# Loading the first batch's k through SyncE in float32 and casting it on the engines, with a new written order, in a kernel of sparse attention and a gated feed-forward

## The chip, the cores and the metric

The kernel runs on one core of one Trainium2 chip. The core has five engines that each follow their own list of instructions: TensorE (PE; its weight loads are shown as PEld), VectorE (DVE), ScalarE (ACT), GpSimd (POOL) and SyncE (SP). Data moves between the chip's memory (HBM) and the core's on-chip memory (SBUF) by DMA, on 16 DMA engines. A DMA is issued by an instruction on POOL or on SP. In this kernel POOL issues every load, and those loads also cast float32 to bfloat16 on the way; SP issues the output stores and small moves inside the core's memory. TensorE writes its results to PSUM.

The metric is the time of one execution in device microseconds (us), the median of several runs.

## The reference

```python
def _attn_ref(q, k, v):                      # B, H, S, D = 4, 8, 768, 64
    block, window = 32, 16
    k_sum = k.reshape(B, H, nb, block, D).max(axis=3)
    v_sum = v.reshape(B, H, nb, block, D).mean(axis=3)
    scores_l = scale * q @ k^T               # kept only where |i - j| < window
    scores_s = scale * q @ k_sum^T + log(block)
    a = softmax over both together
    return a @ concatenate([v, v_sum])
def _moe_ref(x, w_in, w_out):                # x: 3072 x 512, w_in: 512 x 2048
    h = x @ w_in
    return (h * clip(h + 3, 0, 6) / 6) @ w_out
```

Each position attends to the keys less than 16 places away, and to one summary key (the maximum) and one summary value (the mean) of each of the 24 blocks of 32 positions. The heads' outputs are put side by side, and the 3072 rows of 512 go through a feed-forward part with a gated hidden layer of 2048. Inputs and output are float32; the matmuls run in bfloat16.

## The kernel before

**Attention.** Heads go in pairs (four pairs p per batch). For a tile t of 64 queries, the keys are a window of 96 positions and the 24 summary keys, 120 in all. `kaug[p]` holds the transposed keys of pair p by tile, `qT` the transposed queries, `vaug` the values. Scores are computed in halves of six tiles, ACT takes the exponential into `at`, DVE multiplies by a mask (or PE adds a bias first), PE multiplies by the values, DVE normalizes, and PE transposes the result into `x`.

**The first batch.** Batch 0 has its own path. `load_k` (L303) loads k of one or two pairs into `knat` with a casting DMA issued by POOL; 96 partitions hold 8 successive positions of each head. `load_q` (L309) does the same for half of q. Both lie in the tile `first`. `k_step` (L383) transposes k of one pair on PE, DVE takes the block maximum, and ACT or DVE copy the windows into `kaug`. The other half of q comes through `qwide` (`load_wide`, L316): four DMAs. The values come through `load_v` (L339), one DMA per pair. Batches 1 to 3 are loaded in another layout into `kraw`, `qraw` and, for batch 2, again into `first`.

**Feed-forward.** The 3072 rows are eight tiles s of 384. For each, sixteen chunks ft of 128 hidden units: PE multiplies four times (L666), ACT makes the gate (L670), DVE multiplies (L671) into `g`. Then `f2` multiplies `g` by `w_out` (L683), ACT or DVE copy the result out of PSUM, and SP stores it. `w_in` is loaded in five pieces (`load_w`, L371; tokens I0, I2, I4, I8, I12, each holding the chunks from that number up to the next piece: two chunks in I0 and I2, four in the others), `w_out` in four (`load_w2`, L376; tokens O0 to O3). They stay on chip.

**The order.** Nothing is scheduled by the engines themselves. The kernel lists its operations with their dependencies, and a long text, `ORDER`, says in which order they are issued; each engine takes its own in that order. A token such as `k1.2:A` is the operation number 2 of the step k1, put on ACT (`:D` is DVE). The step letters that matter here: K0p load k of pair p; Q0g load q; V0p load values; Q0wu load wide q; k and q the steps that transpose them; s0ph scores of batch 0, pair p, half h; u block sums of the values; h halo copies of values; v0p the values' product for pair p; Fsxft the hidden chunk ft of row tile s (for the first five chunks of tile 0 its four matmuls are four operations, .0 to .3); Gstsx0 the second product; c the constants. Tokens that start with `_`, `-`, `~` or `=` are dummy matmuls on a tile of ones, which fill time in which PE would otherwise be idle (40 of 64 columns for `_40`, 15 of 128 for `-15`, 12 of 512 for `~12`, one of 64 times n for `=n`).

A transfer is waited for by the engine whose next instruction needs it. DMAs issued by POOL share eight completion counters in turn, so that each also waits for the eighth DMA before it.

Of the kernel before, what the change touches and what calls it, by code (L numbers as in the profile page):

```python
# [29 lines left out]
c.0 K00.0 c.7 c.17 c.6 c.8:A K01.0 c.10:D c.5 c.1 _40 -15 k0.0 k0.2:A c.18 ~1 =2 k1.0 K02.0 ~12 =3 k2.0 k3.0 c.15:D c.2 c.3  # L30
s000.0 k0.3:A c.13:D c.4 c.11:A k1.1 Q00.0 q0.0 k1.4 k0.1 c.20 k1.2:A Q01.0 ~2 =5 q1.0 k0.4 k1.3:D c.9:A c.14:A c.19 k2.3:A
q0.1:A s000.1 q0.2:A =1 s010.0 s010.1 k2.2:A k3.2:D k3.3:D k3.1 V00.0 h000.0:D h001.0:D k2.1 k2.4 s000.2 ~2 =5 v00.0 V01.0 u0.0
h010.0:D s020.0 c.16 s010.2 q1.2:A u0.3:D u0.1:D u0.4:D v01.0 v01.1 v01.2 v00.1 q1.1:A V02.0 h020.0:A h021.0:A h011.0:A v00.2
s020.1 v01.3 v00.3 V03.0 u1.0 u1.3:A h030.0:D s030.0 k3.4 ~2 s030.1 u1.4:D v01.4 h031.0:D Q0w0.0 Q0w1.0 v01.5:D Q0w2.0 =1 q3.0
q3.1:D q2.0 u1.1:A u1.2:D s020.2 v02.0 v02.1 v02.2 s021.0 v02.3 s030.2 v03.0 v03.1 q2.1:A v03.2 s011.0 v03.3 v00.4 v00.5:D v02.4
s021.1 s011.1 s021.2 v03.4 v03.5:D s011.2 v02.5:A s031.0 s031.1 s001.0 s031.2 I2.0 F0x3.0 F0x3.1 F0x3.2 F0x3.3 F0x3.4 F0x3.5
I4.0 F0x6.0 F0x6.1 F0x6.2 F0x4.0 F0x4.1 F0x4.2 F0x4.3 v411.0 v411.1 F0x5.0 F0x4.4 F0x4.5 v411.2 s001.1 I8.0 u0.2:A s001.2 F0x8.0
F0x8.1 F0x8.2 F0x5.1 I0.0 F0x5.2 F0x11.0 F0x1.0 F0x11.1 F0x11.2 F0x1.1 F0x1.2 F0x1.3 F0x1.4 F0x1.5 v410.0 v410.1 F0x7.0 F0x7.1
F0x7.2 v410.2 F0x10.0 F0x10.1 I12.0 F0x13.0 F0x13.1 F0x15.0 F0x15.1 F0x13.2 F0x10.2 v411.3 v411.4:D v410.3 v410.4:A F0x15.2
F0x14.0 F0x14.1 F0x14.2 F0x9.0 F0x9.1 F0x9.2 F0x0.0 F0x0.1 F0x2.0 F0x2.1 K13.0 K10.0 c.12:A F0x0.2 K12.0 K11.0 w10.0 Q1w1.0  # L40
F1x14.0 F1x14.1 F1x14.2 F1x4.0 F1x4.1 F1x4.2 F1x2.0 F1x2.1 F1x2.2 w10.1:D F0x2.2 F0x2.3 F0x2.4 F0x12.0 F0x12.1 F0x12.2 F1x8.0
F1x8.1 F1x8.2 F1x1.0 F1x1.1 F1x1.2 F0x0.3 F0x0.4 F0x0.5 F0x2.5 F1x9.0 F1x9.1 F1x9.2 F1x5.0 F1x5.1 F1x5.2 F1x15.0 F1x15.1 w11.0
w11.2 F1x15.2 w11.3:D Q1w4.0 Q1w2.0 Q1w0.0 w10.2 w10.3:D q6.0 q6.1:A q7.0 q7.1:A F1x7.0 F1x7.1 w11.1:A F1x7.2 F1x12.0 F1x12.1
F1x12.2 O0.0 G02x0.0 Q1w5.0 Q1w3.0 q4.0 q4.1:A q5.0 q5.1:A F1x6.0 F1x6.1 F1x6.2 O1.0 G02x0.1 s100.0 s100.1 s100.3 F1x3.0 w12.0
F1x11.0 F1x11.1 w13.0 w13.2 F1x3.1 F1x11.2 w12.2 w12.1:D O2.0 G02x0.2 s101.0 s101.1 O3.0 F1x10.0 G02x0.3 G02x0.4:A w13.3:D
w13.1:A s101.3 F1x0.0 G00x0.0 G00x0.1 w12.3:D s100.2 s101.2 s100.4 V10.0 h100.0:D F1x10.1 h110.0:A F1x10.2 F1x3.2 s110.0 s110.1
s110.2 s101.4 s110.3 G00x0.2 G00x0.3 G00x0.4:A V12.0 u4.0 h130.0:D h120.0:A F1x0.1 u4.1:D u4.2:A u4.4:D u4.3:D u4.5:D G02x0.5
G01x0.0 G01x0.1 G01x0.2 s110.4 F1x0.2 h111.0:A v100.0 v100.1 v100.2 h121.0:A v101.0 v101.1 v101.2 G01x0.3 G01x0.4:A K20.0 K21.0
K22.0 K30.0 K23.0 w21.0 F1x13.0 F1x13.1 F1x13.2 v100.3 v100.4:A w20.0 w21.3 G12x0.0 w21.2:A v101.3 v101.4:A V22.0 H2.0 h101.0:A
w20.3 G12x0.1 G12x0.2 F2x2.0 F2x2.1 F2x11.0 F2x2.2 F2x11.1 F2x11.2 s111.0 w23.0 s111.3 F2x1.0 F2x1.1 F2x1.2 F2x3.0 F2x3.1 F2x3.2  # L50
F2x15.0 F2x15.1 F2x15.2 Q22.0 w23.3 G12x0.3 s111.1 G12x0.4:A F2x5.0 F2x5.1 h131.0:A F2x5.2 F2x6.0 G10x0.0 s111.2 w22.0 w22.3
s111.4 w23.4:A V20.0 H2.1:A K33.0 F2x13.0 F2x13.1 F2x13.2 G10x0.1 F2x6.1 F2x0.0 F2x0.1 F2x0.2 u5.0 u5.1:A u5.5:A F2x6.2 v110.0
v111.0 v111.1 v111.2 Q30.0 F2x4.0 F2x4.1 F2x4.2 Q21.0 Q23.0 Q20.0 w22.4:A F2x10.0 F2x10.1 F2x10.2 F2x12.0 F2x12.1 w20.1 F2x12.2
w22.2:A v110.1 w21.4:A Q33.0 Q32.0 G10x0.2 G01x0.5 G10x0.3 G10x0.4:A v110.2 F2x8.0 F2x8.1 w21.1 w20.2:A F2x9.0 w20.4:A F2x9.1
F2x9.2 u5.2:D F2x14.0 u5.4:D w23.2:A F2x8.2 v111.3 F2x14.1 v111.4:A G11x0.0 G11x0.1 u5.3:D w22.1 v110.3 v110.4:A F2x7.0 F2x7.1
G11x0.2 F3x14.0 F3x14.1 F2x14.2 F2x7.2 F3x14.2 s200.0 s200.1 w23.1 w21.5:A s200.3 G11x0.3 F3x9.0 F3x9.1 F3x9.2 F3x8.0 F3x8.1
F3x8.2 F3x13.0 Q31.0 K31.0 s200.4 s200.2 G11x0.4:A G11x0.5 G12x0.5 s210.0 s210.3 s210.4 s210.1 s210.2 F3x4.0 F3x12.0 G22x0.0
# [104 lines left out]
def kernel(  # L162
# [535 lines left out]
    load_q(0)
    load_k(0, 1)
    load_k(1, 2)  # L700
    load_q(1)
    load_k(2, 4)
# [100 lines left out]
```

## Time and profile before

| what | value |
|---|---|
| median of 3 runs | 217.12 us (217.12 to 217.85) |
| profiled execution | 217.01 us, its span 215.3 us |
| PE busy | 209.4 us, 97% of the span |
| DVE, ACT, POOL busy | 162.5, 136.2, 49.5 us |
| first matmul of the feed-forward part | 24.33 us after the start |
| landed through queue 0 (POOL's loads) | 14.41 MB |
| landed through queue 1 (SP's stores and moves) | 7.87 MB |

The span is the time between the first and the last instruction that the profiler recorded. A row of the timeline has the start, the duration, the engine, the line, the operation, what it writes and reads, and in brackets how long the engine had been idle before and what ended that. In a row by stretches, the numbers after the stretch's length are the busy time of PE, PEld, DVE, ACT and POOL (each with a count of instructions), then the granted clock of PE, how much the DMA engines had in flight, and the GB/s that landed. A GB/s line divides a stretch into 40 slices. In the chain of work that ended last, each row is a start, a duration and what was running. In the groups, the numbers after the bar are busy time and the mean duration of one in ns.

### The profile page before, as it was taken

How to read it: one execution, taken by the hardware profiler on the slowest of the kernel's cores; microseconds unless marked ns; L12 is line 12 of the kernel's file. 1: busy time of each engine (PE TensorE's matmuls, PEld its weight loads, DVE VectorE, ACT ScalarE, POOL GpSimd, SP SyncE). 2: the span in 40 equal slices, each digit the busy share in tenths (PEclk: the TensorE clock that was granted, in tenths of full speed). 3: DMA queues.
4: the chain of work that ended last, by engine and by line, in shares of the span. 5: the costliest groups of instructions: out<-in, count | busy, mean ns of one | idle time of the engine just before them, and what ended most of it. 6: DMA issues, size and time to landing. Idle time of an engine off the chain costs nothing.

```text
span 215.3 us, 6088 instructions
## 1 busy us (share of the span) xinstructions
PE 209.4 (97%) x2548; PEld 119.6 (56%) x2548; DVE 162.5 (75%) x317; ACT 136.2 (63%) x264; POOL 49.5 (23%) x66
## 2 busy tenths in 40 slices
PE   7998999999999999999999999999999999999993
PEld 7556656555555565555555555555555555565442
DVE  6888999999899999898889888987865554640021
ACT  3887878887898988757569696466345355520110
POOL 7977358906652244000000000000000000000000
PEclk9999999999999999999999999999999999999999
DMA  5999999999999999930333233122323300013124
GB/s 74 157 152 188 203 188 170 191 204 161 205 160 192 181 134 150 104 146 12 37 43 137 28 38 107 49 24 32 73 56 48 73 0 29 23 49 122 52 70 150
DMA packets 91580, 22.68 MB, mean 105 GB/s; under 512 B 82208, under 2 KB 88608, under 8 KB 91552
## 3 DMA queue, kind: packets, MB, share of 16 engines
q0 software_dynamic: 62288, 14.41, 72.2%
q1 hardware_dynamic: 29264, 7.87, 15.4%
q8 instruction: 20, 0.33, 0.6%
q14 instruction: 8, 0.07, 0.1%
HBM read 28.82 MB, written 6.29 MB: 163 GB/s over the span
## 4 chain that ended last, share of the span: by engine, by line
PE 86%; DMA 7%; POOL 2%; ACT 2%; DVE 1%; issue 1%; ACTq 0%; POOLq 0%
PE h L666 38%; PE o L683 33%; PE h L683 5%; DMA qwide<-in_q_dram 4%; DMA first<-in_q_dram 3%; PE S L623 3%; PE S L512 3%; PE S L553 1%; ACT vaug L241 1%; POOL first L305 1%; PE S L636 1%; PE S L439 1%; PE S L666 1%; PE h L581 1%; DVE g L671 0%
## 5 line engine op out<-in xcount | busy, mean ns | idle before, releaser
L666 PE MATMUL h<-x,win 128*128 128x384 bf16 x500 | 91.1, 326 | 0.2 <-DVE g L671 0.2
L670 ACT ACTIVATE r<-h 128x384 f32<-128x384 f32 x125 | 58.8, 492 | 38.7 <-PE h L666 36.7
L671 DVE SCALAR_TENSOR_TENSOR g<-r,h 128x384 bf16<-128x384 f32 x125 | 65.7, 546 | 22.7 <-ACT r L670 20.1
L683 PE MATMUL o<-wout,g 128*128 128x512 bf16 x336 | 81.7, 379 | 0.0
L666 PEld LDWEIGHTS <-win 128*128 128x128 bf16 x512 | 48.7, 98 | 35.8 <-issue 0.4
L683 PEld LDWEIGHTS <-g 128*128 128x128 bf16 x400 | 38.4, 98 | 37.6 <-issue 0.3
L520 ACT ACTIVATE at<-S 120x768 bf16<-120x768 f32 x24 | 18.6, 811 | 5.5 <-PE S L512 5.4
L241 ACT COPY ot<-o 128x512 f32<-128x512 f32 x17 | 10.0, 586 | 16.3 <-PE o L683 15.1
L521 DVE TENSOR_TENSOR at<-at,mask 96x768 bf16<-96x768 bf16 x24 | 12.6, 549 | 2.0 <-ACT at L520 1.6
L605 DVE TENSOR_TENSOR xn<-S,rc 128x768 bf16<-128x768 f32 x14 | 13.3, 949 | 0.3
L241 DVE COPY ot<-h 128x512 f32<-128x512 f32 x2 | 1.3, 686 | 14.1 <-PE h L683 14.1
L343 POOL DMA_DIRECT2D vaug<-in_v_dram x10 | 11.8, 1187 | 0.3 <-issue 0.2
L683 PE MATMUL h<-wout,g 128*128 128x256 bf16 (+1 forms) x64 | 11.4, 326 | 0.0
L467 DVE TENSOR_REDUCE red<-kaug 128x24 bf16<-128x768 bf16 x12 | 11.2, 941 | 0.1
L241 ACT COPY vaug<-vs 24x1536 bf16<-24x1536 bf16 x6 | 8.8, 1468 | 0.6 <-DVE vs L241 0.5
L241 ACT COPY vaug<-vaug 32x640 bf16<-32x640 bf16 (+3 forms) x17 | 8.9, 574 | 0.3 <-PE S L553 0.2
L771 PE MATMUL o<-idle 128*128 128x64 bf16 (+2 forms) x70 | 7.4, 286 | 1.1 <-DVE idle L287 1.1
L455 DVE STREAM_TRANSPOSE kaug<-kraw 128x768 bf16<-128x768 bf16 x8 | 8.1, 1020 | 0.3 <-PE S L512 0.3
L333 POOL DMA_DIRECT2D kraw<-in_k_dram x8 | 5.9, 741 | 9.1 <-DVE kaug L455 7.3
L642 DVE STREAM_TRANSPOSE y<-xn 128x768 bf16<-128x768 bf16 x8 | 7.6, 965 | 0.2
L512 PEld LDWEIGHTS <-kaug 32*128 32x128 bf16 x576 | 5.3, 92 | 4.4 <-issue 3.6
L623 PEld LDWEIGHTS <-at 120*64 120x64 bf16 x336 | 6.2, 111 | 2.6 <-issue 1.5
(106 smaller groups left out, 184.2 us busy)
## 6 DMA issues: line engine op xcount, KB each, us to landing
out_dram<-ot SPq DMA_DIRECT2D x19, 256.0 KB, 2.3
vaug<-in_v_dram POOLq DMA_DIRECT2D x6, 384.0 KB, 12.9
wout<-in_moe_w_out_dram POOLq DMA_DIRECT2D x4, 512.0 KB, 9.9
win<-in_moe_w_in_dram POOLq DMA_DIRECT2D x3, 512.0 KB, 10.7
kraw<-in_k_dram POOLq DMA_DIRECT2D x8, 192.0 KB, 12.7
x<-y SPq DMA_DIRECT2D x64, 24.0 KB, 2.0
first<-in_k_dram POOLq DMA_DIRECT2D x6, 192.0 KB, 12.4
first<-in_q_dram POOLq DMA_DIRECT2D x6, 192.0 KB, 12.3
```

Of the source, the lines that this page charges most:

```text
L241: {"ACT": nc.scalar.copy, "DVE": nc.vector.tensor_copy, "POOL": nc.gpsimd.tensor_copy}[eng](o, i)
L343: op("POOL", "dma128", lambda: nc.gpsimd.dma_start(out=o[BLK:WIN, a:z, 0:D], in_=rows[:, a:z]), w=[("v", b % 2, c) for c in range(lo, hi)] ...
L467: op("DVE", "max", lambda: nc.vector.tensor_reduce(red.slot[:], w[:, :, BLK:WIN].rearrange("p t (n c) -> p t n c", n=2), axis=AX.X, op=ALU ...
L512: nc.tensor.matmul(X[g // 2].slot[:, g % 2, i * QB:(i + 1) * QB], kaug[2 * u + m][rows, t], qT[rows, 2 * u + m, t * QB:(t + 1) * QB], star ...
L520: op("ACT", "exp", lambda a=a, e=e: nc.scalar.activation(a, X[e].slot[0:KEYS, :, 0:HALF], AF.Exp, scale=scl), r=[X[e]], w=[("at", p, half)])
L521: op("DVE", "masking", lambda m=m: nc.vector.tensor_tensor(m, m, mask[:, low(half):low(half) + HQ].unsqueeze(1).to_broadcast([WIN, 2, HQ, ...
L605: nc.vector.tensor_tensor(o, src[..., 0:D], r.unsqueeze(len(r.shape)).to_broadcast(list(o.shape)), op=ALU.mult)
L623: nc.tensor.matmul(X.slot[64 * c:64 * c + 64, i, m:m + D + 1], a[:, t * QB:(t + 1) * QB], vaug[b % 2][0:KEYS, h, t, 0:D + 1], start=True, ...
L666: nc.tensor.matmul(bank(h)[:, 0:HALF], w_in_sb[:, kt, cols], xt[s].slot[:, kt], start=(kt == 0), stop=(kt == NP - 1))
L670: op("ACT", "relu", lambda: nc.scalar.activation(r.slot[:], bank(h)[:, 0:HALF], AF.Relu, bias=0.5, scale=1.0 / 6.0), r=[h], w=[r])
L671: op("DVE", "gate", lambda: nc.vector.scalar_tensor_tensor(gt[s].slot[:, ft], r.slot[:], 1.0, bank(h)[:, 0:HALF], op0=ALU.min, op1=ALU.mul ...
L683: nc.tensor.matmul(o.slot[:, a:z], gt[s].slot[:, ft, ts * 128:(ts + 1) * 128], w_out_sb[:, ft, a:z], start=(ft == 0), stop=(ft == NFT - 1))
```

## The change

k of batch 0 no longer comes through POOL's casting DMAs. SP loads it in float32, one DMA per pair, into memory that belongs to `w_out_sb` (named `kgiven` there; w_out is loaded later). Then eight new operations, one per head, cast it into `knat`: five on DVE and three on ACT in the new order. `k_step` waits for the casts of its two heads. The loads of w_out wait until the casts have read their source, and the later loads into `first` wait as before for what reads `knat`.

```diff
+    kgiven = w_out_sb[0:RP].rearrange("p f m -> p (f m)").bitcast(F32).rearrange("p (h x) -> p h x", h=H)
...
-    def load_k(lo, hi):
-        plan.at(f"K0{lo}")
-        op("POOL", "dma1024", lambda: nc.gpsimd.dma_start(
-            out=knat[:, 2 * lo:2 * hi], in_=k[0, 2 * lo:2 * hi].rearrange("h (p s) d -> p h s d", s=RUN)),
-           w=[("kn", p) for p in range(lo, hi)], size=192 * (hi - lo))
+    def load_k(p):
+        plan.at(f"K0{p}")
+        op("SP", "kfirst", lambda: nc.sync.dma_start(
+            out=kgiven[:, 2 * p:2 * p + 2], in_=k[0, 2 * p:2 * p + 2].rearrange("h (r s) d -> r h (s d)", s=RUN)),
+           w=[("kg", p)], size=2)
+        for h in (2 * p, 2 * p + 1):
+            op(EITHER, "kcast", lambda eng, h=h: copy(eng, knat[:, h].rearrange("p s d -> p (s d)"), kgiven[:, h]), r=[("kg", p)], w=[("kn", h)])
...
-           w=[("wout", c)], size=512)
+           w=[("wout", c)], size=512, free=[("kg", p) for p in range(NP)])
...
-        op("PE", "ktr", tr, r=[("kn", p), "ident"], w=[T])
+        op("PE", "ktr", tr, r=[("kn", 2 * p), ("kn", 2 * p + 1), "ident"], w=[T])
```

`ORDER` is new from the first token to the last. Its start, up to the first matmuls of the feed-forward part, before:

```
c.0 K00.0 c.7 c.17 c.6 c.8:A K01.0 c.10:D c.5 c.1 _40 -15 k0.0 k0.2:A c.18 ~1 =2 k1.0 K02.0 ~12 =3 k2.0 k3.0 c.15:D c.2 c.3
s000.0 k0.3:A c.13:D c.4 c.11:A k1.1 Q00.0 q0.0 k1.4 k0.1 c.20 k1.2:A Q01.0 ~2 =5 q1.0 k0.4 k1.3:D c.9:A c.14:A c.19 k2.3:A
...
s021.1 s011.1 s021.2 v03.4 v03.5:D s011.2 v02.5:A s031.0 s031.1 s001.0 s031.2 I2.0 F0x3.0 F0x3.1 F0x3.2 F0x3.3 F0x3.4 F0x3.5
I4.0 F0x6.0 F0x6.1 F0x6.2 F0x4.0 F0x4.1 F0x4.2 F0x4.3 v411.0 v411.1 F0x5.0 F0x4.4 F0x4.5 v411.2 s001.1 I8.0 u0.2:A s001.2 F0x8.0
F0x8.1 F0x8.2 F0x5.1 I0.0 F0x5.2 F0x11.0 F0x1.0 F0x11.1 F0x11.2 F0x1.1 F0x1.2 F0x1.3 F0x1.4 F0x1.5 v410.0 v410.1 F0x7.0 F0x7.1
F0x7.2 v410.2 F0x10.0 F0x10.1 I12.0 F0x13.0
```

and after (whole, up to the same place):

```
c.0 Q01.0 c.6 c.10:A c.11:A Q00.0 c.8:D c.20 c.7 c.13:A c.14:A c.5 c.15:D c.9:D c.18 K00.0 K00.2:A c.19 K01.0 K01.2:D K00.1:A
c.1 -33 q1.0 q1.2:A K01.1:D =3 k1.0 k1.2:A k1.3:A c.16 V00.0 V01.0 c.17 K03.0 K03.1:D K03.2:D k0.0 k0.1 q0.0 q0.1:D c.2 c.3 ~6
=5 s010.0 k1.1 k1.4 K02.0 K02.2:D k0.4 s000.0 =1 k3.0 k3.1 h000.0:D k0.3:A q0.2:A s010.1 k0.2:A q1.1:A c.4 =7 s000.1 u0.0
h010.0:D K02.1:A k2.0 s000.2 v00.0 u0.1:A v00.1 k2.2:D V02.0 h020.0:A u0.3:D s010.2 k2.1 s030.0 ~3 =3 s020.0 V03.0 u1.0 k3.2:A
k3.3:A k2.3:A k2.4 =3 s020.1 v00.2 k3.4 h011.0:D v00.3 Q0w0.0 Q0w2.0 Q0w1.0 q2.0 s030.1 q2.1:D =4 q3.0 s020.2 u1.3:A I12.0
q3.1:D v01.0 v01.1 v02.0 u1.4:D v01.2 u1.1:A v01.3 s030.2 s011.0 v02.1 v02.2 h030.0:D v02.3 v00.4 v00.5:D s011.1 u0.4:A s011.2
s001.0 s001.1 ~1 =5 s031.0 s031.1 v03.0 v03.1 v03.2 v03.3 =1 s021.0 s021.1 v01.4 v01.5:D v02.4 v02.5:D v03.4 v03.5:A h001.0:A
u1.2:D I0.0 F0x0.0 I4.0 F0x4.0 F0x4.1 s021.2 s031.2 h021.0:D F0x0.1 F0x4.2 F0x0.2 I2.0 F0x3.0 F0x3.1 F0x3.2 F0x4.3 F0x4.4 F0x4.5
F0x13.0 F0x13.1 F0x13.2 F0x0.3 F0x0.4 F0x0.5 F0x15.0 I8.0 F0x3.3 F0x15.1 F0x15.2 F0x3.4 F0x3.5 F0x12.0 F0x12.1 F0x12.2 F0x10.0
```

On POOL this gives the order q, q, the identity matrix, v, v, the band, v, v, wide q in four DMAs, then I12, I0, I4, I2, I8, where it was k, k, the identity, k, the band, q, q, four of v, wide q, then I2, I4, I8, I0, I12. On SP the four loads of k (pairs 0, 1, 3, 2) stand first.

More of the change, by code (lines that the diff above doesn't have):

```diff
@@ L29 @@
 ORDER = """
[L30 to L57, printed above, removed]
@@ new lines @@
+s001.2 F0x10.1 F0x10.2 h031.0:A F0x1.0 F0x1.1 F0x1.2 F0x1.3 F0x7.0 F0x7.1 F0x7.2 F0x11.0 F0x11.1 F0x11.2 u0.2:A v411.0 v411.1
+F0x2.0 F0x2.1 F0x2.2 F0x2.3 F0x2.4 v411.2 F0x2.5 F0x14.0 F0x14.1 F0x14.2 F0x1.4 F0x5.0 F0x5.1 v410.0 c.12:A O0.0 K12.0 K10.0
+F0x8.0 F0x8.1 K11.0 v410.1 F0x1.5 v410.2 F0x9.0 F0x9.1 F0x9.2 F0x5.2 F0x8.2 v411.3 v411.4:A G02x0.0 v410.3 v410.4:A Q1w2.0
+Q1w1.0 Q1w0.0 q6.0 q6.1:A F0x6.0 F0x6.1 K13.0 w13.0 w11.0 F1x5.0 F1x6.0 F1x5.1 F1x5.2 F0x6.2 F1x6.1 F1x6.2 w11.2 q7.0 q7.1:A
@@ new lines @@
+v111.3 G10x0.3 G10x0.4:A w20.1 F2x2.0 w23.4:D w22.4:A v111.4:A w22.1 F2x1.0 w22.2:A G11x0.0 F2x2.1 F2x14.0 F2x14.1 F2x14.2
+G11x0.1 G11x0.2 F2x1.1 w22.5:A K31.0 K30.0 F2x1.2 F2x2.2 w23.2:A w23.1 s200.0 s200.3 s200.4 F2x11.0 F3x10.0 s200.1 F3x12.0
+F3x10.1 F3x10.2 s210.0 F2x11.1 F2x11.2 s200.2 G11x0.3 s210.3 s210.4 s210.1 s210.2 F2x6.0 F2x6.1 F2x6.2 w21.5:A F3x12.1 F2x7.0
+F2x7.1 F3x12.2 G12x0.5 G10x0.5 G00x0.5 G01x0.5 v201.0 F2x7.2 v201.1 v201.2 v201.3 v200.0 v200.1 v200.2 v200.3 G11x0.4:A w20.5:A
@@ L86 @@
+F7x11.2 G60x0.0 G71x256.0 G71x256.1 G71x0.0 G71x256.2 G71x0.1 G71x256.3 G71x256.4:A G70x0.0 G70x0.1 G60x0.1 G60x0.2 G60x0.3
+G70x0.2 G60x0.4:A G50x0.0 G50x0.1 G50x0.2 G70x0.3 G42x0.5 G50x0.3 G50x0.4:D G71x256.5 G72x0.0 G72x0.1 G60x0.5 G62x0.5 G70x0.4:A
+G72x0.2 G72x0.3 G61x0.0 G50x0.5 G61x0.1 G61x0.2 G61x0.3 G71x0.2 G71x0.3 G72x0.4:D G72x0.5 G70x0.5 G61x0.4:D G61x0.5 G71x0.4:A
+G71x0.5
 """
@@ L336, in load_raw @@
                    w=[(name + "r", b % 2, g)], size=768,
-                   free=[(n, p) for p in range(NP) for n in ("kn", "qn")] if b == 2 else [("qw", 1, u) for u in range(NS)] if b == 3 else ())
+                   free=[("kn", h) for h in range(H)] + [("qn", p) for p in range(NP)] if b == 2 else [("qw", 1, u) for u in range(NS)] if b == 3 else ())
     def load_v(b, lo, hi):
@@ L696, in f2 @@
             op("SP", "store2" if n else "store", store, r=[ot], size=z - a)
[L698 to L702, printed above, removed]
+    for p in range(NP):
+        load_k(p)
+    for g in range(2):
+        load_q(g)
     for c in range(NP):
```

64 lines of the change are left out of this document (36 added, 28 removed).

## The prediction, made before the changed kernel ran

> **What bounds the kernel now.** I read the page first (shares, slices, queues), then busy time by stretches, then the chain that ended last, then POOL's timeline.
>
> ```profile
> span 215.3 us, 6088 instructions
> PE 209.4 (97%) x2548; PEld 119.6 (56%) x2548; DVE 162.5 (75%) x317; ACT 136.2 (63%) x264; POOL 49.5 (23%) x66
> ...
> PE   7998999999999999999999999999999999999993
> ...
> DMA  5999999999999999930333233122323300013124
> ...
> q0 software_dynamic: 62288, 14.41, 72.2%
> ...
> HBM read 28.82 MB, written 6.29 MB: 163 GB/s over the span
> ```
> ```profile
> 2.00:3.00 1.00, 1.00 (x24) 1.00 (x22) 0.79 (x2) 0.94 (x2) 0.99 (x3) 1.00 0.17 17
> ```
> ```profile
> 3.00:10.00 7.00, 7.00 (x91) 4.58 (x90) 5.84 (x20) 4.10 (x8) 6.79 (x12) 1.00 1.15 155
> 10.00:17.00 7.00, 6.71 (x163) 4.25 (x157) 5.94 (x17) 6.06 (x15) 5.34 (x8) 1.00 2.34 156
> 18.00:28.00 10.00, 9.25 (x189) 6.14 (x184) 8.96 (x23) 8.27 (x14) 5.26 (x8) 1.00 1.33 204
> ```
> ```profile
> 160.00:190.00 30.00, 30.00 (x171) 16.48 (x169) 16.99 (x31) 14.90 (x32) 0.00 (x0) 1.00 0.18 38
> 190.00:215.30 25.30, 21.85 (x119) 11.31 (x116) 3.64 (x6) 3.22 (x7) 0.00 (x0) 0.98 0.27 94
> ```
> ```profile
> 12.48 7.88 DMA qwide<-in_q_dram
> ...
> 20.40 0.73 PE h L441 x10
> 21.13 0.61 PE h L581 x24
> 21.75 0.28 PE S L489 x12
> ...
> 23.53 0.34 PE h L589 x3
> ...
> 24.33 2.06 PE h L666 x12
> ...
> 211.93 0.37 ACT ot L241
> ```
>
> TensorE is busy 97% of the span, and from the first matmul of the feed-forward part (24.33) on it has almost no gap until the last copy (211.93). What lies after 24.33 is a fixed amount of matmul work, so the time moves with one number: when that stream starts and can run on. Before 24.33 the chain is DMA: the wide q lands at 20.36 (12.48 + 7.88), then 3.97 us of dependent PE work.
>
> The DMA is a stream, not a latency. Queue 0 (POOL's casting loads) begins near 2.9: the stretch 2 to 3 moved 17 GB/s against 155 afterwards. The GB/s column counts landed bytes (14.41 MB landed of 28.82 MB read), so k, q and v come at 310 GB/s read, the later loads at 408.
>
> ```profile
> 1.36 1.42 POOL L305 DMA_DIRECT2D first<-in_k_dram  x2 [0.84 <-POOLq L787]
> ...
> 3.31 0.73 POOL L305 DMA_DIRECT2D first<-in_k_dram  x1
> ...
> 4.76 1.33 POOL L312 DMA_DIRECT2D first<-in_q_dram  x2
> 6.08 3.76 POOL L343 DMA_DIRECT2D vaug<-in_v_dram  x4
> ...
> 16.85 1.48 POOL L373 DMA_DIRECT2D win<-in_moe_w_in_dram  x2 [0.51 <-DMA vaug<-in_v_dram]
> ...
> 20.64 0.71 POOL L333 DMA_DIRECT2D kraw<-in_k_dram  x1 [0.70 <-DMA qwide<-in_q_dram]
> 21.89 0.72 POOL L333 DMA_DIRECT2D kraw<-in_k_dram  x1 [0.54 <-issue]
> 24.03 0.89 POOL L325 DMA_DIRECT2D qraw<-in_q_dram  x1 [1.42 <-DMA win<-in_moe_w_in_dram]
> ...
> 26.56 0.88 POOL L325 DMA_DIRECT2D qraw<-in_q_dram  x1 [1.64 <-DMA win<-in_moe_w_in_dram]
> 27.88 0.88 POOL L325 DMA_DIRECT2D qraw<-in_q_dram  x1 [0.44 <-DMA win<-in_moe_w_in_dram]
> 30.43 0.54 POOL L324 DMA_DIRECT2D qraw<-in_q_dram  x1 [1.67 <-DMA win<-in_moe_w_in_dram]
> ```
>
> POOL keeps eight DMAs in flight (each issue waits for the eighth before it), so these waits date the landings: the last v at 16.85, I2 by 21.89, I4 24.03, I8 26.56, I0 27.88, I12 30.43. A megabyte read of `win` costs 2.5 us (I4 to I8).
>
> **The change, part by part.** Let d be how much earlier the stream behind k, q, v and wide q lands.
>
> *New order of the `win` loads.* Before, after wide q: I2 (256 KB landed), I4 (512), I8 (512), I0 (256), I12 (512). Now I12, I0, I4, I2, I8. By bytes ahead, I0 takes the place that I4 had, I4 that of I8, I2 that of I0, I8 that of I12. So I0 lands at 24.03 - d, I4 at 26.56 - d, I2 at 27.88 - d, I8 at 30.43 - d. On PE the order is now F0x0.0, F0x4.0, F0x4.1, F0x0.1, F0x4.2, F0x0.2, F0x3.0. F0x4 needs I4; F0x3 needs I2 and has six matmuls ahead, 1.03 us at 2.06/12. The stream can therefore stand as if begun at 27.88 - 1.03 - d = 26.85 - d, against 24.33. (F0x10 needs I8 with 24 matmuls ahead, 4.1 us: 26.3 - d, which doesn't bind.) **The change pays only if d is over 2.5 us.** Before, the first chunk needed was the first to land, so nothing of this sort waited.
>
> *What PE does ahead of that.* The work before the first F is the same set, but s030.1 (0.28), v01 (0.61 and its transposes, 0.34 at most) and dummies of 1,152 columns (0.49, at 2.85/13 per 512) now stand behind wide q: 3.97 + 1.7 = 5.7 us after it, so at 26.1 - d. Then F0x4's wait begins: this path hides behind the loads by 0.3 us at F0x4 (after F0x0.0) and 0.8 at F0x3.
>
> ```profile
> 0.91 0.17 DVE L287 MEMSET idle<- 128x128 bf16 x1 [0.91 <-PEq L787]
> ...
> 1.13 3.92 PE L771 MATMUL o<-idle 128*128 128x64 bf16 x55 [1.13 <-DVE idle L287]
> ...
> 6.80 2.85 PE L771 MATMUL o<-idle 128*128 128x512 bf16 x13
> ```
> ```profile
> 91.71 1.30 SPq L694 DMA_DIRECT2D out_dram<-ot  x3
> ```
> ```profile
> GB/s 3 109 0 0 0 0 0 0 0 0 0 0 0 0 0 0 41 328 382 410 396 328 382 423 396 328 383 423 396 341 273 14 0 0 0 0 0 0 0 0
> ```
> ```profile
> GB/s 179 182 179 182 177 182 172 184 179 187 172 223 269 323 361 264 346 294 328 335 302 243 185 177 328 172 164 175 164 169 168 166 163 168 173 160 165 169 164 168
> ```
>
> *k on SP.* No load on SP is in the trace; the nearest rows are SP's stores. The first GB/s line is 90 to 96 us in 0.15 us slices: three stores (256 KB each) with nothing beside them, issued from 91.71, moving from about 92.5 to 94.65, so 0.8 us to the first byte and 0.79 MB in 2.1 us, 370 GB/s. The second is 56 to 60 us in 0.1 us slices: one store beside POOL's loads. In the eleven raised slices 0.33 MB moved, 0.26 of it the store's, so the loads fell from 180 to some 60 GB/s. Alone, the store would take 0.7 us and the loads' part 0.4: together the 1.1 us seen. The engines are shared in time; nothing is free.
>
> So d has two terms. Lead: SP can issue when the other engines start (0.91), first bytes near 1.7 instead of 2.9: 1.2 us. Rate: k is 1.57 MB read, 5.1 us at 310 GB/s before, 4.2 us at 370: 0.85 us. Less about 0.1 for mixing, d = 1.95. Bounds: the lead alone, 1.2, or 0 if float32 loads run at the 240 GB/s that the store got beside loads (k 6.6 us); above, 5.1 if k cost POOL's stream nothing. I take 1.95, since both store rows point there. At d = 1.95 the new order loses 2.5 - 1.95 = 0.55 us.
>
> The Trainium skill, "DMA: Bandwidth & Descriptors", section "Issuing engines are not separate DMA queues", speaks against the change: DMAs from SP, ACT and GpSimd run on the same 16 engines and interleave, so several issuers only save the sequencer's issue time. The 56 to 60 line agrees about sharing. By that rule alone d would be the lead, and the time that of the first rival.
>
> *POOL* loses three issues (1.42 + 0.73 us); q moves from 4.76 to 1.36 and v from 6.08 to some 3.3. This is worth nothing by itself: q then queues in the same engines beside k.
>
> ```profile
> L241 ACT COPY ot<-o 128x512 f32<-128x512 f32 x17 | 10.0, 586 | 16.3 <-PE o L683 15.1
> ```
> ```profile
> L241 DVE COPY ot<-h 128x512 f32<-128x512 f32 x2 | 1.3, 686 | 14.1 <-PE h L683 14.1
> ```
> ```profile
> L241 DVE CAST vf<-o 24x128 bf16<-24x128 f32 x2 | 0.6, 294 | 0.0
> ```
>
> *Eight casts* of 96x512, five on DVE and three on ACT: between 0.29 us (a 128 column cast) and 0.69 (512 float32 columns), say 0.5 each, 2.5 us of DVE and 1.5 of ACT. DVE's two for k3 stand ahead of the block maximum of k0, so a late k3 holds k0 and k1 too. Cover: all k should have landed near 7 to 8 us, while the last v lands at 16.85 - d = 14.9 and wide q at 18.4; cost nothing. With d above 3.5 that cover is gone and about 0.7 to 1.4 us of casts shows.
>
> *Dummies* fall from 80 to 52 (15,296 to 11,392 columns): they only fill waits, so nothing. *w_out's memory* is lent to k until the casts end, near 8; `wout` is loaded after `win`: nothing. The rest of the order is new too; PE had no idle to give back between 24.33 and 211.9, so I take 0, with 0.5 either way.
>
> Sum: the profiled execution took 217.01 (span 215.3 and 1.7 around it); 217.01 + 0.55 = 217.6. The median shown is 217.12, so +0.2%. I call half a per cent, 1.1 us, the least that can be told from no change.
>
> **Rivals.** *Only the lead (slower).* float32 doubles the bytes written, so k on SP may run no faster than the cast did: d = 1.2, time 217.01 + 1.3 = 218.3; at d = 0, 219.5. For it: SP's store got only 240 GB/s beside loads. Against: 370 alone. It decides below d = 1.4. *k beside POOL's loads for nothing (faster).* 310 read against 408 later leaves a quarter of the engines' rate unused until 17 us, and the new order, with its `win` chunks in this sequence and fewer dummies, fits such a world. At d = 5.1 F starts at 21.8: 217.01 - 2.5 = 214.5, more likely 215.3 with the casts showing. If only the unused quarter is filled (3.93 MB of k, q, v at 408: 9.6 us instead of 12.7, and the lead), d = 4.3: 215.2. It decides above d = 3.6. Against: the store slices, where the loads lost what the store gained.
>
> **Chances.** Forecast (d from 1.4 to 3.6): 0.45, its own range 215.9 to 218.1. Only the lead, or less: 0.35. For nothing: 0.2. The range reaches into both, to 215.2 and 219.2. So faster 0.2, same 0.45, slower 0.35.
>
> **What would show it.** The first F matmul beyond F0x0.0 should start near 24.6, after a PE wait of about 0.3 us on a DMA into `win`, and another of some 0.5 before F0x3; wide q landing near 18.4; the GB/s of the first 5 us well above before; POOL's waits for `win` dated 1.95 earlier by place. Wrong, if wide q lands before 16.8 (then faster) or after 19 (slower), if PE waits on k's casts instead of `win`, or if gaps open after 40 us, from the new order.

## The result, and the profile after

| | before | after |
|---|---|---|
| median | 217.12 us (217.03 to 217.85) | 223.03 us (222.69 to 223.79) |
| profiled execution, its span | 217.01, 215.3 us | 223.79, 222.0 us |
| first scores on PE | 12.70 us | 18.40 us |
| first matmul of the feed-forward part | 24.26 us | 30.84 us |

The changed kernel is slower: the ratio is 1.027, with a 95% interval of 1.0243 to 1.0297. The prediction was 217.6 us, with a range from 215.2 to 219.2. The medians and ranges below count every execution, while the ratios leave out those over 1.5% above the fastest of the same kernel. The date of the first matmul of the feed-forward part is read from PE's timeline (in the chain it is 24.33 before). All the kernels below compute the whole reference; none leaves work out.

The page of the kernel after, its span, PE's busy tenths and the granted clock in 40 slices of 5.55 us:

```profile
span 222.0 us, 6024 instructions
...
PE   6199999999999999999999999999999999999993
...
PEclk9658999999999999999999999999999999999999
```

The second slice has PE at a tenth and the clock at six tenths. Before, those digits were 9 and 9. What differs lies there and just behind it. The two ends of the feed-forward stream, first in the timeline of PE in the kernel after, then in that of the kernel before (start, duration, operation; the last row of each is the last matmul):

```profile
30.84 0.33 PE L671 MATMUL S<-x,win 128*128 128x384 bf16 x1
...
217.33 1.04 PE L688 MATMUL h<-wout,g 128*128 128x256 bf16 x8
```
```profile
24.26 2.12 PE L666 MATMUL h<-x,win 128*128 128x384 bf16 x12
...
210.81 1.04 PE L683 MATMUL h<-wout,g 128*128 128x256 bf16 x8
```

From the first F matmul to the end of the last matmul it is 187.5 us after (218.37 - 30.84) and 187.6 before (211.85 - 24.26). So nearly the whole of the 6.7 us that the span grew is a start that comes 6.58 us late.

The chain that ended last in the first 31 us of the kernel after (start, duration, what was running):

```profile
1.36 9.14 DMA first<-in_q_dram
...
10.54 0.85 PE o L425 x16
...
11.67 1.42 PE h L396 x32
13.09 0.64 PE h L425 x16
13.73 2.94 PE S L775 x7
16.67 1.28 PE S L486 x4
...
18.51 0.96 DVE red L407
...
27.49 0.81 ACT at L500
```

It begins with one DMA of 9.14 us: q. After it there is no DMA at all before the feed-forward part; PE, DVE and ACT work hand in hand to the end. Before, the chain passed through two DMAs (q, then wide q). What the wait does to PE shows in PE's timeline and in the busy times by stretches of 4 us (PE, PEld, DVE, ACT, POOL, each with its count, then the granted clock):

```profile
2.70 1.93 PE L775 MATMUL o<-idle 128*128 128x128 bf16 x18
10.54 0.85 PE L425 MATMUL o<-ident,first 96*64 96x96 bf16 x16 [5.92 <-DMA first<-in_q_dram]
...
13.66 3.01 PE L775 MATMUL S<-idle 128*128 128x512 bf16 x7
16.46 1.49 PE L486 MATMUL S<-bias,ident 96*128 96x384 bf16 x4
...
18.40 0.35 PE L494 MATMUL S<-qT,kaug 64*128 64x64 bf16 x12
```
```profile
4.00:8.00 4.00, 0.63 (x8) 0.45 (x6) 2.70 (x8) 2.17 (x4) 3.86 (x7) 0.96 1.05 219
8.00:12.00 4.00, 1.46 (x27) 1.17 (x29) 0.76 (x2) 0.48 (x1) 2.28 (x4) 0.50 1.77 199
12.00:16.00 4.00, 4.00 (x50) 2.43 (x47) 2.83 (x6) 3.18 (x10) 2.74 (x4) 0.50 2.43 155
16.00:20.00 4.00, 3.76 (x60) 2.10 (x59) 1.98 (x4) 1.32 (x3) 3.59 (x6) 0.76 1.82 184
```

PE has nothing to do from 4.63 to 10.54, and the granted clock falls to 0.50 and stays there beyond 16 us, over work that is on the chain: the seven dummies (six of 512 columns, one of 320) take 3.01 us; at a clock of 1.0 the same seven take 1.60 (the row is shown below, with both repairs).

What landed in the first 8 us, by queue, after and then before (packets, MB, busy share of the DMA engines):

```profile
q1 hardware_dynamic: 661, 1.26, 62.9%
q0 software_dynamic: 346, 0.17, 16.7%
```
```profile
q0 software_dynamic: 842, 0.79, 72.0%
```

Queue 0 is POOL's: q and v after, k, q and v before, its first DMA issued at 1.36 us in both. Beside k on queue 1 it landed 0.17 MB by 8 us, against 0.79. q was issued first on POOL and its halves still landed at 10.5 (q1) and 12.0 (q0), about where they landed before behind all of k (q0 by 10.8, q1 at 12.2). Moving k to SP did not bring q earlier.

The dates at which POOL saw the last v and then I0, I4, I2 and I8 land, in its timeline after:

```profile
16.90 1.48 POOL L378 DMA_DIRECT2D win<-in_moe_w_in_dram  x2 [0.41 <-DMA vaug<-in_v_dram]
...
23.74 1.01 POOL L330 DMA_DIRECT2D qraw<-in_q_dram  x1 [1.08 <-DMA win<-in_moe_w_in_dram]
25.88 0.88 POOL L330 DMA_DIRECT2D qraw<-in_q_dram  x1 [1.13 <-DMA win<-in_moe_w_in_dram]
27.26 0.54 POOL L329 DMA_DIRECT2D qraw<-in_q_dram  x1 [0.50 <-DMA win<-in_moe_w_in_dram]
29.71 0.83 POOL L330 DMA_DIRECT2D qraw<-in_q_dram  x1 [1.91 <-DMA win<-in_moe_w_in_dram]
```

By place that is 0.05 later than before at v (16.85), and 0.29, 0.68, 0.62 and 0.72 earlier at `win`. So d was about 0 to 0.7. And it did not matter: I4 and I2 lay ready 5.0 and 3.6 us before the first F matmul.

### The profile page after: what moved, and what is told of

It reads as the page before. It is cut to its first block, busy times and chain, and to the rows that moved or that the text cites. A ratio compares the mean times of both kernels' runs of the same rounds, so it can differ in the third digit from the quotient of the medians.

```text
span 222.0 us, 6024 instructions
## 1 busy us (share of the span) xinstructions
PE 208.2 (94%) x2494; PEld 120.4 (54%) x2520; DVE 161.9 (73%) x309; ACT 138.6 (62%) x280; POOL 47.7 (21%) x63
## 3 DMA queue, kind: packets, MB, share of 16 engines
HBM read 28.82 MB, written 6.29 MB: 158 GB/s over the span
## 4 chain that ended last, share of the span: by engine, by line
PE 90%; DMA 4%; DVE 2%; issue 1%; ACT 1%; DVEq 0%; POOLq 0%
PE h L671 37%; PE o L688 32%; PE h L688 5%; DMA first<-in_q_dram 4%; PE S L628 3%; PE S L517 3%; PE S L775 1%; PE S L558 1%; PE S L641 1%; PE S L671 1%; PE h L396 1%; PE S L444 1%; ACT at L500 1%; PE h L775 1%; PE S L486 1%
## 5 line engine op out<-in xcount | busy, mean ns | idle before, releaser
L688 PE MATMUL o<-wout,g 128*128 128x512 bf16 x310 | 78.3, 379 | 2.0 <-issue 1.0
L525 ACT ACTIVATE at<-S 120x768 bf16<-120x768 f32 x24 | 18.7, 809 | 5.1 <-PE S L517 4.9
L243 DVE COPY ot<-o 128x512 f32<-128x512 f32 x4 | 2.8, 690 | 14.1 <-PE o L688 14.1
L243 ACT COPY ot<-h 128x256 f32<-128x256 f32 (+1 forms) x3 | 1.3, 444 | 14.4 <-PE h L688 14.4
L243 ACT COPY vaug<-vaug 32x640 bf16<-32x640 bf16 (+2 forms) x16 | 8.7, 583 | 0.3 <-PE S L558 0.2
L500 ACT ACTIVATE at<-S 120x768 bf16<-120x768 f32 x8 | 6.3, 811 | 3.6 <-PE S L494 3.5
L775 PEld LDWEIGHTS <-idle 128*128 128x128 bf16 x52 | 5.3, 134 | 4.3 <-issue 2.3
```

The lines of the kernel that those rows point to most:

```text
L243: {"ACT": nc.scalar.copy, "DVE": nc.vector.tensor_copy, "POOL": nc.gpsimd.tensor_copy}[eng](o, i)
L525: op("ACT", "exp", lambda a=a, e=e: nc.scalar.activation(a, X[e].slot[0:KEYS, :, 0:HALF], AF.Exp, scale=scl), r=[X[e]], w=[("at", p, half)])
L688: nc.tensor.matmul(o.slot[:, a:z], gt[s].slot[:, ft, ts * 128:(ts + 1) * 128], w_out_sb[:, ft, a:z], start=(ft == 0), stop=(ft == NFT - 1))
```

## The experiments

Unless said otherwise the edit is one of `ORDER`, and only its start is shown.

**Keep PE busy through the wait for q.**

```diff
-c.1 -33 q1.0 q1.2:A K01.1:D =3
+c.1 -33 ~26 q1.0 q1.2:A K01.1:D =3
```

> The changed kernel with 26 more dummies of 512 columns (some 5.7 us) ahead of q1.0, where PE stood idle for 5.9 us; nothing else differs. Theory 'half clock' (the idle wait put PE on half its clock from 7.5 to 18 us, and the work behind q, 7.7 us of it, ran at half speed): that work takes some 4 us less, s010.1 moves from 18.4 to about 15, F starts some 3 us earlier, 220 us. Rival 'queue' (q lands at 10.5 at the head of PE's list, and the waits behind it do the rest): the clock is full but F starts less than 1 us earlier, 222 to 223.

Measured: 220.95 us (220.32 to 222.07), ratio 1.0165 (1.0109 to 1.022), 2.1 us less than the change. The page's clock line and the start of the stream:

```profile
PEclk9999999999999999999999999999999999999999
```
```profile
28.81 0.33 PE L671 MATMUL S<-x,win 128*128 128x384 bf16 x1
```

26 useless matmuls made the kernel faster: the idle stretch had also cost half speed for what follows it. The gain is two thirds of what was expected. The first scores start at 16.26 and not near 15, since q0 landed only at 13.1 in this execution and PE waited 1.20 us for it.

**Do PE's work on k first.** k0 and k1 land before q does, but stood behind q1 in PE's list.

```diff
-q1.0 q1.2:A K01.1:D =3 k1.0 k1.2:A k1.3:A ... K03.2:D k0.0 k0.1 q0.0
+K01.1:D =3 k1.0 k1.2:A k1.3:A ... K03.2:D k0.0 q1.0 q1.2:A k0.1 q0.0
```

> The changed kernel with k1.0 and k0.0 ahead of q1.0 on PE (and q's first copy behind theirs on ACT). Theory 'queue': k is transposed, copied and reduced while q is on its way, s010.1 needs only q and moves from 18.4 to about 16 (q0.0 and the dummies are still there, and PE still idles some 3 us before q), 220.5 to 221. Theory 'half clock': PE still cools, so less than 1 us is gained, 222 to 223.

Measured: 222.07 us (221.03 to 222.49), ratio 1.0204 (1.0153 to 1.0254). The first F matmul starts at 28.18 in the profiled execution, which took 221.03 us, the fastest of its runs. The scores start at 15.89, as the first theory had it; the median is in the range of the second. The clock still falls (PE waits 2.77 us for the casts of k, then for q), so a part of the loss is left.

**Take away the dummies behind q.**

```diff
-c.2 c.3 ~6 =5 s010.0
+c.2 c.3 s010.0
```

> The changed kernel without the seven dummies (~6 =5) between q0.0 and s010.0, which took 3.0 us at half clock. If they stood on the path: s010.1 is then bound by DVE's k1.4, which ended near 16, and moves from 18.4 to about 16.3; F up to 2 us earlier, 221. If the path is elsewhere (DVE's chain, the values): no change, 223.

Measured: 225.88 us (224.36 to 227.91), ratio 1.0383 (1.0281 to 1.0485). The page's clock line:

```profile
PEclk9755799999999999999999999999999999999999
```

Neither expectation held: with less work the kernel is slower (ratio 1.0383 against 1.027, though the two intervals overlap at their ends). Without the seven long dummies PE has a gap at the covers (1.04 us), and the clock comes back at 25.1 instead of 17.9. The scores start earlier (16.67 against 18.40), yet the first F matmul later (31.60 against 30.84). Being busy did not bring the clock back by itself, as the busy times from 14.5 to 25 us show (PE busy 10.50 of 10.50 us, granted clock 0.50):

```profile
14.50:25.00 10.50, 10.50 (x142) 6.82 (x141) 7.76 (x20) 6.46 (x16) 6.44 (x9) 0.50 1.62 190
```

**The route alone: the order of before, k by SP, each cast just ahead of its transposes.**

```diff
-c.0 K00.0 c.7 c.17 ... K01.0 ... k0.0 ... k1.0 K02.0 ~12 =3 k2.0 k3.0
+c.0 K00.0 K01.0 K02.0 K03.0 c.7 c.17 ... K00.1:A K00.2:D k0.0 ... K01.1:A K01.2:D k1.0 ~12 =3 K02.1:A K02.2:D K03.1:A K03.2:D k2.0 k3.0
```

> The order of before with k loaded by SP and cast (the route alone): the four loads of k at the head, each pair's two casts just ahead of its transposes, one head or both on ACT and DVE, all else as before. Theory 'k on SP moves the stream by nothing' (d from 0 to 0.7 as measured): wide q lands at 19.7 to 20.4, F starts at 23.7 to 24.5, 216.5 to 217.5. The prediction's term (d = 1.95): wide q at 18.4, F near 22.5 to 23, 215 to 215.7. If k's casts hold the path: 218 or more.

Measured: 225.92 us (222.58 to 226.11), ratio 1.0308 (1.02 to 1.0415). The profiled execution took 226.07 us, so I read only the start of its chain, with the DMA that ends it:

```profile
2.23 7.79 DMA wout<-in_k_dram
```

k2 and k3 are all there only at 10.0, and DVE's casts of them block the constants and maxima that stand behind them on DVE. This build mixes the route with that block, so it does not price the route.

**k alone on the engines.** POOL is held by a copy of one element until all of k has landed; q and v are issued after it. In `ORDER` SP's four loads and the copy stand first.

```diff
+    op("POOL", "hold", lambda: nc.gpsimd.tensor_copy(held[:], kgiven[0:1, H - 1, 0:1]), r=[("kg", p) for p in range(NP)])
```

> The changed kernel with one tiny POOL copy ahead of q's loads that reads the last k, so that POOL issues nothing until all four loads of k have landed: this measures k on SP with nothing beside it, and is of no use otherwise. The prediction's rate (370 GB/s, as SP's stores alone): 1.57 MB in 4.2 us from 1.7, so all k landed and q issued by about 6.5 to 7. Rival 'float32 loads of 96 partitions are slow by themselves' (200 to 250 GB/s): 8 to 9.5. Where the first holds, the slowness seen beside q (k landed near 10) is from sharing.

The hold's row and the GB/s (last column) by stretches, with nothing beside k:

```profile
7.85 0.43 POOL L707 COPY held<-wout 1x1 f32<-1x1 f32 x1 [7.33 <-DMA wout<-in_k_dram]
```
```profile
2.00:4.00 2.00, 2.00 (x22) 2.00 (x21) 1.47 (x8) 1.99 (x4) 0.00 (x0) 1.00 0.89 283
4.00:6.00 2.00, 0.84 (x8) 0.57 (x6) 1.34 (x4) 2.00 (x4) 0.00 (x0) 1.00 0.98 259
6.00:8.00 2.00, 0.00 (x0) 0.00 (x0) 1.11 (x5) 0.17 (x1) 0.15 (x1) 1.00 0.90 229
```

Even alone, SP's float32 loads of k move 229 to 283 GB/s: 1.57 MB by 7.85, in about 5.9 us, on average some 270. The stores of 370 GB/s were no measure for them. POOL's casting loads took k, q and v at 310 read, so by bytes read k on SP is the slower way, not the faster one. (One execution, 225.04 us: q is late by design here.)

**The route with the late casts moved back:** the order of before, k by SP, q ahead on POOL, the casts of k2 and k3 behind DVE's other early work, two more dummies.

```diff
+c.0 K00.0 K01.0 K02.0 K03.0 Q00.0 Q01.0 c.7 ... c.14:A c.19 K02.1:A K02.2:D K03.1:A K03.2:D ~14 =3 k2.0 k3.0
```

> The order of before with k loaded by SP and q first on POOL, and the casts of k2 and k3 placed behind the work of DVE and ACT that doesn't need them, with two more dummies there so that PE doesn't idle: the route without the casts in the way and without cooling. 'The stream moves by 0 to 0.7 and that is all': F starts at 23.7 to 25, 216.5 to 218. If the late k2 and k3 (landed near 10) and the casts still hold the path: F at 26 or later, 219 or more. The prediction's d of 1.95: 215 to 215.7.

Measured: 219.83 us (219.67 to 221.66), ratio 1.0118 (1.0072 to 1.0165). POOL's dates for `win`, in the places of before:

```profile
23.94 0.89 POOL L330 DMA_DIRECT2D qraw<-in_q_dram  x1 [2.20 <-DMA win<-in_moe_w_in_dram]
26.54 0.88 POOL L330 DMA_DIRECT2D qraw<-in_q_dram  x1 [1.70 <-DMA win<-in_moe_w_in_dram]
27.65 0.88 POOL L330 DMA_DIRECT2D qraw<-in_q_dram  x1 [0.23 <-DMA win<-in_moe_w_in_dram]
```

Against 24.03, 26.56 and 27.88 that is a lead of 0.02 to 0.23 us: the earlier start of SP's loads buys the stream next to nothing. F starts at 26.69, as expected for the case that casts still hold the path, and they do. The chain runs from the load of k1 (landed at 6.17) through its cast and other work of DVE and ACT to a cast of k2 that ACT ends at 12.52, and k2's transposes start at 12.56. The clock fell as well (0.67 from 8 to 12 us). So this build doesn't price the route free of blocks either.

**The change with both repairs:** k ahead of q on PE, and 22 dummies around it.

```diff
-c.1 -33 q1.0 q1.2:A K01.1:D =3 k1.0 ... K03.2:D k0.0 k0.1 q0.0
+c.1 -33 ~12 K01.1:D =3 k1.0 ... K03.2:D k0.0 ~10 q1.0 q1.2:A k0.1 q0.0
```

> The changed kernel with both repairs: k1.0 and k0.0 ahead of q1.0 and enough dummies (12 and 10 of 512 columns) to keep PE busy until q lands. If clock and PE's list are the whole loss, F is bound by the win loads as the prediction had it (26.85 less 0.3 to 0.7): F at 26.2 to 26.6, 219 to 219.5. If the gains of the two don't add, because the chain of values behind is as long: 220.5 to 221.

Measured: 220.55 us (219.59 to 220.94), ratio 1.0125 (1.0084 to 1.0166), clock 1.0 throughout the profiled execution. In PE's timeline:

```profile
10.74 0.53 PE L425 MATMUL o<-ident,first 96*64 96x96 bf16 x16 [0.22 <-DMA first<-in_q_dram]
12.05 0.53 PE L425 MATMUL h<-ident,first 96*64 96x96 bf16 x16 [0.78 <-DMA first<-in_q_dram]
12.51 1.60 PE L775 MATMUL S<-idle 128*128 128x512 bf16 x7
...
27.39 0.33 PE L671 MATMUL S<-x,win 128*128 128x384 bf16 x1
```

F starts 3.45 us earlier than in the change, and 3.1 later than before. What is left waits for q, and for a path of engine work behind it.

**The order alone:** the new order, with k by POOL's casting loads at the places of its tokens.

```diff
-K00.0 K00.2:A c.19 K01.0 K01.2:D K00.1:A c.1 -33 q1.0 q1.2:A K01.1:D =3
+K00.0 c.19 K01.0 c.1 -33 q1.0 q1.2:A =3
```

> The new order with k loaded by POOL's casting DMAs, each at the place where the new order has the load of its pair (the order alone: q, q, k0, k1, identity, v, v, k3, band, ...). k0 and k1 then land near 9 to 10 and k2 last of all, behind v; if the new order needs k early (it was written for k on SP), 223 or more. If the loss of the change is SP's loads taking the DMA engines from q, q lands at 5 to 6 here, and the time is below the changed kernel's: 219 to 221.

Measured: 220.8 us (220.0 to 221.57), ratio 1.0143 (1.0106 to 1.018). In PE's timeline:

```profile
5.24 0.53 PE L420 MATMUL o<-ident,first 96*64 96x96 bf16 x16 [0.41 <-DMA first<-in_q_dram]
...
9.79 1.49 PE L391 MATMUL h<-ident,first 96*64 96x96 bf16 x32 [3.82 <-DMA first<-in_k_dram]
...
28.39 0.33 PE L666 MATMUL S<-x,win 128*128 128x384 bf16 x1
```

With k off SP, q1 lands by 5.24 instead of 10.5. This is the direct evidence that k's loads on SP held q back. But k is now late, PE waits 3.82 us for it, and the clock falls here too.

**One pair of k on SP,** the order of before, the other three by POOL; and **two pairs.**

```diff
-c.0 K00.0 c.7 c.17 ... -15 k0.0
+c.0 K00.0 c.7 c.17 ... -15 K00.1:A K00.2:D k0.0
```

> The kernel before, in its old order, with only the first pair's k (K00) loaded by SP and cast, one head on ACT and one on DVE just ahead of k0's transposes; the other k stays with POOL's casting DMAs. It asks whether the lead alone can be kept: SP's first bytes come near 1.9 instead of 2.9, and 0.39 MB runs at 270 instead of 310. 'The lead is kept' (d near 0.8): wide q at 19.5, F at 23.5, 216.3. 'SP's load only takes from POOL's' (d near 0): 217 to 217.5. If k0's casts delay k0 and the order behind it: 218.

> As the run before it, with two pairs (K00 and K01) by SP and the last two by POOL. 'The lead is kept': d near 0.65, 216.4. 'Every k on SP costs': slower than with one pair, 217.5 to 219, since q and the last k on POOL then wait for SP's second load as well.

Measured: one pair 217.38 us (216.97 to 218.96), ratio 1.0001 (0.9983 to 1.0019): no change. Two pairs 218.09 us (217.4 to 220.25), ratio 1.0037 (1.0013 to 1.006). With one pair, F starts at 24.20 against 24.26. No share of k on SP brings a gain. Whether the small loss with two pairs comes from the bytes stays open, for its executions spread from 217.4 to 220.25, and in the profiled one, the longest, PE worked at about half speed for a while. The 13 dummies that take 2.85 us in the kernel before took 5.19, although the clock is recorded as 1.00 in that stretch:

```profile
8.48 5.19 PE L782 MATMUL o<-idle 128*128 128x512 bf16 x13
```
```profile
8.00:12.00 4.00, 4.00 (x23) 1.68 (x20) 3.80 (x14) 3.12 (x7) 3.28 (x5) 1.00 1.95 166
```

So a recorded clock of 1.00 doesn't rule out half speed.

**Fill the wait with real work:** the repaired change, with the covers and k3 ahead of q on PE, and the maxima of k0 and k1 ahead of k3's casts on DVE.

```diff
-K03.0 K03.1:D K03.2:D k0.0 ~10 q1.0 q1.2:A k0.1 q0.0 ... ~6 =5 s010.0 k1.1 k1.4 K02.0 ... s000.0 =1 k3.0
+K03.0 K02.0 k0.0 ... k1.1 k0.1 k1.4 k0.4 ~7 s010.0 s000.0 K03.1:D K03.2:D =1 k3.0 q1.0 q1.2:A ~3 q0.0
```

> The repaired changed kernel (k ahead of q on PE, kept warm) in which also the seven dummies, the two covers s010.0 and s000.0 and k3.0 stand ahead of q on PE and the maxima of k0 and k1 ahead of k3's casts on DVE, so that nothing but q0.0 stands between q's landing and s010.1. Theory 'the rest of the loss is what stands behind q': s010.1 moves from 15.2 to near 12.8 and the path to F from 27.5 to near 25.1. Then the win loads bind, as the prediction's order term had it: I4 at 26.1 and I2 at 27.4, F as if begun at 26.3, 219. If the win order costs nothing: 217.8. If the values' chain behind (v, halo, dummies) holds F: 220.5 as in the repaired one.

Measured: 222.09 us (220.82 to 224.0), ratio 1.0225 (1.0179 to 1.0271), worse than the repaired change. In PE's timeline:

```profile
12.33 0.86 PE L396 MATMUL h<-ident,first 96*64 96x96 bf16 x16 [1.95 <-DVE first L243]
12.98 0.54 PE L425 MATMUL o<-ident,first 96*64 96x96 bf16 x16
```

Now k3's transposes wait for their casts, which wait behind the maxima, and q1, landed by 11.15 in POOL's timeline, waits behind k3 until 12.98 (q0 comes at 13.47 here, 1.4 us later than with both repairs, for which I have no cause). The gaps bring the clock down (0.77 from 12 to 16, 0.50 from 16 to 24 us). It is the fault of the change over again, of my own making.

**The order alone, with PE kept busy:** 16 dummies between q1 and k1.

```diff
-c.1 -33 q1.0 q1.2:A =3
+c.1 -33 q1.0 q1.2:A =3 ~16
```

> The new order alone (all k by POOL's casting loads), with 16 more dummies of 512 columns between the transposes of q1 (whose data landed at 5.24 in the run of the order alone) and those of k1 (whose data landed at 9.79), so that PE has no idle stretch of 3.82 us there and the granted clock should not drop to 0.50. Theory A, the order costs time only because its long wait ahead of k1 halves the clock: in the run of the order alone the work from 9.79 on had no gap on PE, and its 1.49 us of k1 transposes, 0.64 us of q1 transposes, 2.94 us of dummies and 0.85 us of covers ran at about half speed, so that at full clock they take about 3 us instead of 5.9; the scores and what follows start 2.5 to 3 us earlier, the first F matmul is at 25.6 to 26.2 instead of 28.55, and the time is 217.5 to 218.5 us, a ratio of 1.001 to 1.006. Theory B, the order's own path costs it (the work of all four heads' pairs ahead of the first F, on DVE and ACT, is longer than in the old order, or waits for v): the clock is 1.0 all through but the first F stays at 27 or later, and the time is 219 us or more, a ratio over 1.009.

Measured: 219.68 us (219.25 to 220.88), ratio 1.012 (1.0093 to 1.0146). In PE's timeline:

```profile
26.02 0.33 PE L666 MATMUL S<-x,win 128*128 128x384 bf16 x1
...
26.84 1.14 PE L666 MATMUL S<-x,win 128*128 128x384 bf16 x4
```

Neither theory came out whole. The clock is 0.998 and F starts 2.4 us earlier than with the order alone, as A had it; the time is B's. The span fell from 219.3 to 217.8; the ratios of the two builds overlap, so the medians alone don't tell them apart. Two things are left of the order: F still starts 1.76 us later than before, and from its start to the end it takes 0.9 us more (188.46 against 187.5). Of that, 0.3 us is a longer row where F0x3 needs I2 (1.14 us for the four matmuls, 0.81 in the kernel after); POOL's timeline has that piece landed by 27.55. Another 0.5 is one wait of PE for DVE later on.

No version beats the kernel before.

## Why the prediction was wrong, step by step

The profiled executions give this table (us; the first scores, the first F matmul and the rest are read from PE's timeline and the span):

| kernel | first scores | first F | between | span | span less first F |
|---|---|---|---|---|---|
| before | 12.70 | 24.26 | 11.56 | 215.3 | 191.0 |
| after | 18.40 | 30.84 | 12.44 | 222.0 | 191.2 |
| k first | 15.89 | 28.18 | 12.29 | 219.3 | 191.1 |
| PE kept busy | 16.26 | 28.81 | 12.55 | 220.4 | 191.6 |
| both repairs | 15.19 | 27.39 | 12.20 | 218.7 | 191.3 |
| order alone | 16.13 | 28.39 | 12.26 | 219.3 | 190.9 |
| order alone, PE kept busy | 13.66 | 26.02 | 12.36 | 217.8 | 191.8 |

*The time moves with the start of the F stream:* right. The last column holds within 0.9 us, through a spread of 6.6 in the start.

*What PE does ahead of that:* this is the step that failed. It let PE's path begin at wide q (5.7 us after it, 26.1 - d) and hide behind `win`. In the new order the path begins at q and k, and from the first scores on it took, in the rows above, 12.20 to 12.55 us of engine work, in which the change's chain waits for no load. Wide q was not on it: the chain above has no DMA after the first. So F came when the path ended, 30.84, and not when `win` had landed. PE's wait for q is not among the signs of being wrong that the prediction named.

The 6.58 us can be laid out by the profiled executions, taken in one sequence; another sequence would share them out otherwise. Order alone with PE kept busy: 1.76 (0.96 until the first scores, 0.80 behind them). Then k on SP, both repairs made: 1.37, since q0 lands at 12.05 and the scores start at 15.19 instead of 13.66; of this the span shows 0.9, as the earlier stream had to wait behind its start, and the medians don't show it (ratios 1.012 and 1.0125). Then the idle PE and its clock: 3.45. The last term can be counted in rows as well: the same transposes (0.85, 1.49, 0.84), dummies (3.01) and covers (1.49) took 0.53, 0.87, 0.53, 1.60 and 0.81 with both repairs, 3.34 us less in all.

*k on SP, rate:* wrong in size and sign. The term had 370 GB/s and 4.2 us; alone it was about 270 and 5.9, against 5.1 before. So it takes 0.8 of the lead of 1.2 us, and d came out at 0 to 0.7, between the lower bound (d = 0) and the lead alone. The store was the wrong row to take the price from. That the engines are shared in time was right, but I drew no consequence for q, most of which came behind k's bytes. The Trainium skill, "DMA: Bandwidth & Descriptors", section "Queues, rings and completion order", says that each DMA engine takes turns between its queues by whole packets. The counts above don't show equal turns: by 8 us queue 1 had 661 packets to queue 0's 346, and with 1.9 KB in each against 0.5 KB, seven times the bytes landed (about 3.7 times the bytes read, as queue 0's loads read two bytes for each that lands: 28.82 MB read for 14.41 landed before). Whether a packet in these counts is a packet in that page's sense, no run shows.

*POOL, "worth nothing by itself":* half right. q's earlier issue gained nothing, but the order of PE's list relied on it: q1 stood first there, and PE sat idle 5.92 us ahead of it.

*Casts cost nothing:* nearly right. They took 0.4 to 0.9 us each, and the late ones of k3 waited for their data until 9.5, some two us later than I had put it. They weren't on the chain of the change. They held PE up in several experiments (k first, both builds of the route, real work in the wait).

*Dummies cost nothing:* wrong. With the seven behind q removed the ratio rose from 1.027 to 1.0383, and with 26 more the median fell by 2.1 us. The Trainium skill, "TensorE: Matmul & The Clock Gate", section "What's actually happening", says that PE runs at half clock after an idle window of about 3.4 us and needs about that long of steady work to come back. The traces agree on the fall: PE was idle from 4.63, and by stretches of 0.1 us the clock went to 0.50 at 7.7, 3.1 us later, with 3.01 us against 1.60 for the same dummies. On the return they don't: PE was busy almost without a gap from 10.54, and the clock came back at 17.9; without the long dummies 10.5 us of gapless work did not bring it back. In the change, with k first and with the order alone it came back 2.8 to 4.3 us after the seven long dummies began. Why the other matmuls did not bring it back, the runs don't show.

The other three executions of the change were recorded with a mean clock of 1.0 and spans of 221.0 to 221.4, only 0.6 to 1.0 us shorter. By the trace with two pairs that record doesn't show full speed; whether PE ran at half speed in those three stays open, and the median with 26 dummies added speaks for it.

*Order of the `win` pieces:* not tested by the change itself, since the loads lay ready. It showed with the order alone and PE kept busy: a loss of 0.3 us at I2 with F at 26.02.

*The rest of the order, 0 ± 0.5:* wrong. With k by POOL at the places of the new order, where k0 and k1 come late, the order costs 1.4%, and 1.2% with PE kept busy.

*The rivals:* "only the lead" was nearest in d (0 to 0.7), but its price of 218.3 to 219.5 was worked out from `win`, which didn't bind. Its mechanism, a slow k on SP, decided through q instead.

## What to carry to other kernels

When a list is reordered, follow each engine's first instruction that needs data, and ask what is idle if that one lands late: here PE's wait of 5.92 us for q, with the half clock behind it, made up 3.45 of the 6.58 us. Take the price of a load from a load of the same kind and layout, not from a store, and ask what the loads beside it lose. Dummies that "only fill waits" also hold the clock; count them as cover. And check a recorded clock against the duration of a known matmul.

## What was not expected of the hardware

SP's float32 loads onto 96 partitions ran at 229 to 283 GB/s alone, below the 370 of its stores and the 310 read of POOL's casting loads. Two loading queues did not share evenly: by 8 us queue 1 had landed 1.26 MB and queue 0, issued from half a microsecond later, 0.17. And a kernel with 26 more dummy matmuls was 2.1 us faster in the median than the same kernel without them (ratios 1.0165 and 1.027, their intervals apart). By stretches of 0.1 us, the time that the recorded clock stayed at 0.50 comes in steps: 3.4 us in the route with the late casts moved back, 6.8 with k first and with the order alone, 10.2 in the change, with k alone and with real work in the wait, 13.7 in the route alone and 17.1 without the seven dummies, each close to a whole multiple of 3.41.
